# Batching two chunks of a spectral filter's last stage at the border of a step

## The chip, the cores and the metric

One core of one Trainium2 chip. The metric is the device time of one execution in microseconds, lower is better; the median of the runs is taken.

## What is computed

A global filter along the sequence (a real Fourier transform of 3008 points, a product with a filter, the inverse transform), and behind it a dense layer with a hard-swish and a second dense layer, all in fp32:

```python
X = np.fft.rfft(x, axis=1)                      # x: (8, 3008, 256)
Y = X * (filt_r + 1j * filt_i)[None, :, :]
x = np.fft.irfft(Y, n=3008, axis=1).reshape(24064, 256)
h = x @ w_in                                    # (256, 2048)
g = h * np.clip(h + 3.0, 0.0, 6.0) / 6.0
return g @ w_out                                # (2048, 256)
```

## The kernel before

**The two parts.** The 24064 tokens are 47 blocks of 512, which the kernel keeps as 256 pairs (a row and its mirror). For each block the dense layers run over eight slices of 256 hidden units. One slice of one block is a *step*; step 8k + p is slice p of block k. The Fourier stages of the next batch are woven between these steps: a hand-made plan (`at`, `plan`, `do`) says which unit runs at which step and at which of five places in it.

**A step.** In step i the kernel computes the hidden layer of slice p of block k (*up*) and the output products of the slice before (*down*). Both use a scheme with seven products in place of eight (a Strassen form). The tiles:

- *up*: PSUM banks `al` and `be`, one buffer each. `up_1` does three products (A11 into `al`, S1 and A12 into `be`), `up_2` S2 into `al` and S4 into `be`, `up_3` S3 into `al`, `up_5` A22 into `al`. In between, ScalarE copies `al` and `be` out, and VectorE forms the hidden values h0 (`up_2b`, L1007) and h1 (`up_3`, L1012); the last quarter of h1 is a ScalarE copy out of `al` (L1021). ScalarE takes the relu (L1026), VectorE the rest of the hard-swish into `g` (L1031), and three operations make the sums of `g` (`g_sums` L1038, L1039, `g_last` L1044).
- *down*: seven products, numbered 1 to 7, accumulate into four banks po0 to po3 (1 and 4 into po0, 2 and 6 into po1, 5 into po2, 7 and 3 into po3) over the eight slices of a block. Products 1, 2, 5 and 7 open their banks at slice 0. The preceding block's sums are taken out of the banks by `out_1` to `out_5`: ScalarE empties po0, VectorE po1 (`out_2`), one half of po3 (`out_3`), po2 (`out_4`, L1143 and L1144) and the other half of po3 (`out_5`, L1148). `out_4` and `out_5` run in the step with p = 1, in which slice 0 of the new block goes down.

All products go through `strips` (L972): two 64-column halves of the array for each.

**The border of a step.** A plain step issues up_1, place 0, down 1, up_2, down 2 and 4, up_3, down 5 and 6, up_5, down 7 and 3. Where a unit of the transform stands in place 3 (`a8_unit`, `b8_unit`, `bi8_unit`, 32-row shape, banks `al`, `be` and both of the pool psF), the step begins with this unit, and the order is another: unit, down 1, 2 and one half of 4, up_1, S2, the rest of 4 and one half of 5, S4, S3, the rest of 5, 6, 7, A22, 3.

**The last stage of the transform.** The last inverse stage makes the dense layers' input. It runs in *chunks* of five groups (`n_five`: 40 matmuls L899 with 48 rows, four tiles of 64 x 64 of the array at once, into two banks of psF) and of one or two groups (`n_unit`: through `strips`). A chunk reads a half of the tile `t4`, loaded from `g_tmp` by `t4_load` (SP queue), and ScalarE copies the result to the ring `xn` (`ring`, L872), which holds three blocks. A batch between the first and the last has seven chunks, q = 0 to 6: six of five groups and one of two. Before, each chunk runs by itself in place 0, behind up_1; a chunk of one or two groups that shares a step with a five uses unused halves of `al` and of po2 (`spare`). When a block is complete, `ready` plans the sums for the tile `xt` that the up products read: on POOL (`t_sums`), or as ScalarE copies and DMA adds on the POOL queue (`t_copy` L953, `t_add` L958).

Of the kernel before, what the change touches and what calls it, by code (L numbers as in the profile page):

```python
# [10 lines left out]
FP32 = mybir.dt.float32  # L11
I32 = mybir.dt.int32
AXT = mybir.ActivationFunctionType
# [14 lines left out]
NA = 47  # L28
NC = 64
KH = 24  # L30
NF = N // 2 + 1
P = 128
# [24 lines left out]
NBLK = B * N // BLK  # L57
NJ = 5
PAIRS = BLK // 2
RING = 3 * PAIRS  # L60
ND = (NJ + 1) * TOK
NX = PAIRS - NJ * NA
ATOM = 2 * KH
# [166 lines left out]
def kernel(  # L230
# [62 lines left out]
    ones = wai[:, HC * NA:].rearrange("p (s n) -> p s n", s=2)  # L293
    edge = wai[:, ds(2 * (NJ + 1) * NA, ND)]
    edges = edge.rearrange("p (j n) -> p j n", n=TOK)
    wi = const.tile([P, 3, NC], FP32, name="wi")
    wi2 = const.tile([P, 2, HC], FP32, name="wi2")
    xs = const.tile([P, 3, XC, D], FP32, name="xs")
    ft_all = const.tile([P, FB * TC, D], FP32, name="ft")
    ft = [ft_all[:, ts(i, TC), :] for i in range(FB)]  # L300
    t4 = const.tile([P, 2 * NJ, D], FP32, name="t4")
    xn = const.tile([P, 2, 2, RING], FP32, name="xn")
    w_all = const.tile([P, NP, 2, 7, P], FP32, name="w_all")
    w_in, w_out = ([w_all[:, p, i, :, :] for p in range(NP)] for i in range(2))
    b12 = const.tile([P, P], FP32, name="b12")
# [230 lines left out]
        nc.sync.dma_start(x0[X0:XR, j:j + n, :].rearrange("p j d -> p (j d)"), raw(x[0], j, [[HC * D, XR - X0], [1, n * D]]))  # L536

    def zt(dh):
        return (xn.rearrange("p a c n -> p (a c n)"), xs.rearrange("p i j d -> p (i j d)"))[dh]

    def copy(dve, to, ps):
        if dve:
# [290 lines left out]
    def pair(i):  # L833
        b, js, o, n = chunks[i]
        return b * HC * NA + o, n
# [28 lines left out]
                                              ap=[[D, KH], [step * 2 * KH * D, m], [1, D]]))  # L864
                    q += m

    def ring(i, a, m_, to, out, src):
        done = 0
        while done < m_:
            r = (chunks[i][0] * HC * NA + to + done) % RING  # L870
            m = min(m_ - done, RING - r)
            nc.scalar.activation(out=out(ds(r, m)), in_=src[:, :, ds(a + done, m)], func=AXT.Copy)  # L872
            done += m

    def ready(i):
        t, n = pair(i)
        k = t // PAIRS
        if (t + n) // PAIRS > k > 0:
            if n_at[i] % NP == 1 and k - 1 in kinds:
                st["xt", k] = xtp.tile([P, 5, PAIRS], FP32, name="xt")  # L880
                b = 4 + (kinds[k - 1] == "x")
                for j, (step, place_) in enumerate(((1, 1), (2, 0), (2, 1), (2, 1), (2, 2), (2, 2), (b, 1), (b, 1))):
                    plan.setdefault((n_at[i] + step, place_), []).append((t_copy if j < 4 else t_add, (k, j % 4)))
            else:
                t_sums(k)


    def n_five(i, ends_step=False):
        b, js, o, n = chunks[i]
        s0 = i % 2 * NJ  # L890
        banks = [psU.tile([P, 512], FP32, name=x) for x in ("al", "be")] if ends_step else [
            psF.tile([P, 512], FP32, name="psn", tag="f") for c in range(2)]
        ps = [t[:, 0:2 * n].rearrange("p (e n) -> p e n", e=2) for t in banks]
        for q, j in enumerate(js):
            for dh in range(2):
                for g in range(2):
                    for c in range(2):
                        r = ds(c * HALF, ATOM)
                        nc.tensor.matmul(ps[c][ts(g, HALF), dh, ts(q, NA)], t4[r, s0 + q, ds(dh * P + g * HALF, HALF)],  # L899
                                         groups[r, j, :], start=True, stop=True)  # L900
        for c in range(2):
            ring(i, 0, n, o, lambda at_: xn[:, :, c, at_], ps[c])
        ready(i)

    def n_unit(i, dh):
        if spare[i]:
            ps = st["po", n_at[i] // NP][2][:, 1, :, :].rearrange("p u m -> p (u m)") if dh else st["al"][:, 256:512]
        else:
            ps = psF.tile([P, 512], FP32, name="psn", tag="f")
        b, js, o, n = chunks[i]  # L910
        for q, j in enumerate(js):
            w = edges[0:2 * ATOM, FIRST.index(j), :] if i >= TAIL and j else ones[0:2 * ATOM, j, :]
            strips(ps[:, ts(q, TOK)], t4[0:2 * ATOM, i % 2 * NJ + q, ts(dh, P)], w, start=not spare[i], stop=True)
        for q, a, m, to in TO.get(i, [(q, 0, NA, o + q * NA) for q in range(len(js))]):
            ring(i, a, m, to, lambda at_: xn[:, dh, :, at_], ps[:, ts(q, TOK)].rearrange("p (c n) -> p c n", c=2))
        if dh:
            ready(i)


    def direct(i):  # L920
# [11 lines left out]
    def n_first():  # L932
        for (c, dh), ps in st.pop("psn").items():
            for q, j in enumerate(chunks[c][1]):
                strips(ps[:, ts(q, TOK)], t4[:, j - 1, ts(dh, P)], edges[:, FIRST.index(j), :], start=False, stop=True)
            to = xn[:, dh, :, 0:PAIRS]
            if c == 0:
                nc.scalar.activation(out=to[:, :, 0:NJ * NA].rearrange("p h (j a) -> p j h a", a=NA),
                                     in_=ps[:, 0:NJ * TOK].rearrange("p (j h a) -> p j h a", j=NJ, h=2), func=AXT.Copy)
                continue  # L940
            nc.scalar.activation(out=to[:, :, NJ * NA:], in_=ps[:, 0:2 * NX].rearrange("p (h a) -> p h a", h=2), func=AXT.Copy)
            nc.scalar.activation(out=xn[:, dh, :, ds(PAIRS, NA - NX)],
                                 in_=ps[:, 2 * NX:TOK].rearrange("p (c a) -> p c a", c=2), func=AXT.Copy)

    def xb(k, d, c):
        return xn[:, d, c, ts(k % 3, PAIRS)]

    F1, F3, F5, F2, F4 = range(5)

    def t_copy(k, j):  # L950
        t, (s0, s1) = st["xt", k], (xb(k, d, 1) for d in range(2))
        f, n, s, scale = ((F1, 2, s0, -1.0), (F5, 1, s0, 1.0), (F2, 1, s1, 1.0), (F4, 1, s1, -1.0))[j]
        nc.scalar.activation(out=t[:, f:f + n, :], in_=s.unsqueeze(1).broadcast_to([P, n, PAIRS]), func=AXT.Copy, scale=scale)  # L953
# [6 lines left out]
    def t_sums(k):  # L960
        t = xtp.tile([P, 5, PAIRS], FP32, name="xt")
        c0, s0, c1, s1 = (xb(k, d, c) for d in range(2) for c in range(2))
        u, v = (t[:, i, :] for i in (F5, F3))
        f1, f2, f3, f4, f5 = (t[:, i, :] for i in (F1, F2, F3, F4, F5))
        for o, x0, x1, op_ in ((f1, c0, s0, ALU.subtract), (u, c0, c1, ALU.add), (v, s0, s1, ALU.add),
                               (f4, u, v, ALU.subtract), (f5, u, v, ALU.add), (f2, c1, s1, ALU.add), (f3, f1, f2, ALU.add)):
            nc.gpsimd.tensor_tensor(out=o, in0=x0, in1=x1, op=op_)
        st["xt", k] = t

    def strips(ps, w, x, **kw):  # L970
        for o in range(0, P, STRIP):
            nc.tensor.matmul(ps[ds(o, STRIP)], w[:, ds(o, STRIP)], x, skip_group_check=True, **kw)  # L972
# [122 lines left out]
    def plain_up(p):  # L1095
        st["g", 0, p] = gp.tile([P, 7, 256], FP32, name="g")
        st["h"] = [psU.tile([P, 512], FP32, name=n) for n in ("al", "be")]
        for i in range(2):
            for d in range(2):
                strips(st["h"][i], w_in[p][:, 2 * d + i, :], xn[:, d, :, 0:PAIRS], start=d == 0, stop=d == 1)  # L1100
            relu(i)
            hswish(0, p, i)

# [96 lines left out]
    def at(step, fn, *a):  # L1200
        plan.setdefault((step, 0 if fn in EARLY else 1 if fn is w_scale else 2), []).append((fn, a))

    with tc.manual_schedule():
# [133 lines left out]
        at(0, wai_load)  # L1337
        at(2, x_load, 1, 2)

        n_at, spare = {0: -2, 1: -2}, {}  # L1340
        kinds = {}
        for n in range(2, B):
            for d, kind in enumerate("caxFFF"):
                kinds[first[n] - 7 + d] = kind

        N_AT = {"c": ((6, 6), (6, 6), (6, 6)), "F": ((1, 1), (1, 1), (6, 6)), "t": ((2, 4), (2, 4), (6, 6))}
        FIVE_AT = {"c": (6, 3, 6), "a": (1, 1, 5), "x": (1, 1, 5), "F": (1, 0, 1), "t": (4, 2, 4)}
        N_FIRST = {0: ((3, 4),), 1: ((), (2, 2), (3, 3)), 2: ((1, 1),), 3: ((1, 1),)}
        in_block = {}
        for i in range(2, len(chunks)):  # L1350
            in_block.setdefault(pair(i)[0] // PAIRS, []).append(i)
        stored = 0
        for i in range(2, len(chunks)):
            k = pair(i)[0] // PAIRS
            head = chunks[i][2] == 0
            same = in_block[k]
            at_, kind = same.index(i) + 1 if len(same) > 1 else 0, kinds.get(k - 1, "t")
            steps = N_FIRST[k - 1][at_] if k - 1 in N_FIRST else (FIVE_AT[kind][at_],) * 2 if len(chunks[i][1]) == NJ else N_AT[kind][at_]
            if head and len(same) == 1:
                steps = (6, 6)  # L1360
            s0, s1 = ((k - 1) * NP + s for s in steps)
            five = len(chunks[i][1]) == NJ
            n_at[i] = s1
            spare[i] = kind == "c" and at_ == 1
            if head:
                stored = s0 - 3 + (k == first[1])
            at(max(stored, n_at[i - 2] + 1), t4_load, i)
            if five:
                at(s1, n_five, i)
                continue  # L1370
            at(s0, n_unit, i, 0)
            at(s1, n_unit, i, 1)

        A_AT = (3, 10, 18, 21)
        SUM_AT = ((-10, -2), (2, 7), (13, 14), (15, 16))
# [219 lines left out]
```

## Time and profile before

| | us |
|---|---|
| median of 3 runs | 2537.55 (2536.87 to 2537.55) |
| the profiled execution | 2537.7 |
| its span, first to last instruction | 2535.8 |
| TensorE busy | 2521.5 |
| VectorE busy | 2012.9 |
| ScalarE busy | 1362.1 |
| GpSimd busy | 422.8 |

A row of the profile gives the line, the engine, the operation, what is written from what, the shape and the count; in the timeline each row begins with the start and the length in us from the start of the span. TensorE's matmul rows count each of the two passes of an fp32 matmul by itself. Matmuls overlap, so the length of one says less than the time from start to start. The granted clock was 1.0.

### The profile page before, as it was taken

How to read it: one execution, taken by the hardware profiler on the slowest of the kernel's cores; microseconds unless marked ns; L12 is line 12 of the kernel's file. 1: busy time of each engine (PE TensorE's matmuls, PEld its weight loads, DVE VectorE, ACT ScalarE, POOL GpSimd, SP SyncE). 2: the span in 40 equal slices, each digit the busy share in tenths (PEclk: the TensorE clock that was granted, in tenths of full speed). 3: DMA queues.
4: the chain of work that ended last, by engine and by line, in shares of the span. 5: the costliest groups of instructions: out<-in, count | busy, mean ns of one | idle time of the engine just before them, and what ended most of it. 6: DMA issues, size and time to landing. Idle time of an engine off the chain costs nothing.

```text
span 2535.8 us, 87287 instructions
## 1 busy us (share of the span) xinstructions
PE 2521.5 (99%) x37890; PEld 2007.3 (79%) x37890; DVE 2012.9 (79%) x3647; ACT 1362.1 (54%) x2836; POOL 422.8 (17%) x558
## 2 busy tenths in 40 slices
PE   8999999999999999999999999999999999999999
PEld 4478787887888788888888878887888878888887
DVE  6978888888787887878878788787887878766666
ACT  4554455555555555555555555555555555555554
POOL 3252111111211112111121111211102111011110
PEclk9999999999999999999999999999999999999999
DMA  8745556554445344443443443534424343211000
GB/s 239 235 123 165 162 138 155 160 136 101 118 98 137 99 102 121 98 129 99 112 121 86 132 109 98 135 89 117 121 68 96 88 103 91 53 41 26 19 22 26
DMA packets 210821, 276.91 MB, mean 109 GB/s; under 512 B 23274, under 2 KB 176392, under 8 KB 210054
## 3 DMA queue, kind: packets, MB, share of 16 engines
q1 hardware_dynamic: 163985, 200.75, 27.0%
q0 software_dynamic: 46112, 70.28, 14.2%
q8 instruction: 297, 4.87, 0.8%
q14 instruction: 86, 0.70, 0.1%
q10 hardware_dynamic: 341, 0.31, 0.1%
HBM read 164.38 MB, written 128.81 MB: 116 GB/s over the span
## 4 chain that ended last, share of the span: by engine, by line
PE 97%; DMA 1%; DVE 1%; SPq 0%; issue 0%; ACT 0%; DVEq 0%
PE po L972 46%; PE al L972 26%; PE be L972 19%; PE psn L899 2%; PE be L608 1%; PE al L779 1%; PE psf L706 1%; DMA bits<-in_moe_w_in_dram 0%; PE psf L693 0%; PE psf L589 0%; DMA w_all<-in_x_dram 0%; PE psf L763 0%; DMA zp_tmp<-y 0%; DMA w_all<-in_filt_r_dram 0%; PE po L685 0%
## 5 line engine op out<-in xcount | busy, mean ns | idle before, releaser
L972 PEld LDWEIGHTS po<-w_all,g 128*64 128x64 f32 x20808 | 1231.1, 137 | 263.0 <-issue 35.4
L972 PE MATMUL po<-w_all,g 128*64 128x128 f32 (+1 forms) x20808 | 1406.8, 274 | 0.3 <-DVE g L1031 0.3
L1026 ACT ACTIVATE r<-h,half_c 128x512 f32<-128x512 f32 x736 | 531.2, 722 | 335.9 <-DVE h L1007 323.8
L972 PE MATMUL al<-xt,w_all 128*64 128x256 f32 x4416 | 663.9, 379 | 0.1
L1031 DVE SCALAR_TENSOR_TENSOR g<-r,h 128x512 f32<-128x512 f32 x736 | 519.4, 706 | 146.9 <-ACT r L1026 133.5
L972 PE MATMUL be<-xt,w_all 128*64 128x256 f32 x2944 | 442.5, 379 | 0.0
L1007 DVE TENSOR_TENSOR h<-be,s 128x512 f32<-128x512 f32 x368 | 253.6, 689 | 169.8 <-PE be L972 138.0
L972 PEld LDWEIGHTS al<-xt,w_all 128*64 128x64 f32 x4416 | 285.1, 137 | 28.9 <-POOL w_all L469 1.0
L972 PEld LDWEIGHTS be<-xt,w_all 128*64 128x64 f32 x2944 | 209.0, 137 | 97.5
L1021 ACT ACTIVATE h<-al 128x256 f32<-128x256 f32 x368 | 141.0, 383 | 266.6 <-PE al L972 264.8
L1039 DVE TENSOR_TENSOR g<-g 128x512 f32<-128x512 f32 x367 | 255.6, 696 | 12.6
L1012 DVE TENSOR_TENSOR h<-al,s 128x256 f32<-128x256 f32 x368 | 155.6, 423 | 138.1 <-PE al L972 137.8
L972 PE MATMUL al<-xn,w_all 128*64 128x256 f32 (+1 forms) x1536 | 236.6, 388 | 1.0 <-DVE g L1031 0.5
L972 PE MATMUL be<-xn,w_all 128*64 128x256 f32 (+1 forms) x1536 | 236.4, 388 | 0.0
L991 ACT ACTIVATE s<-be 128x256 f32<-128x256 f32 x368 | 141.0, 383 | 148.9 <-PE be L972 145.9
L1002 ACT ACTIVATE s<-al 128x256 f32<-128x256 f32 x368 | 141.2, 384 | 124.2 <-PE al L972 121.0
L990 ACT ACTIVATE s<-al 128x256 f32<-128x256 f32 x368 | 141.5, 385 | 82.5 <-PE al L972 82.4
L1038 DVE TENSOR_TENSOR g<-g 128x256 f32<-128x256 f32 x367 | 162.1, 442 | 12.6
L1044 DVE TENSOR_TENSOR g<-g 128x256 f32<-128x256 f32 x367 | 155.4, 423 | 2.3
L972 PEld LDWEIGHTS be<-xn,w_all 128*64 128x64 f32 x1536 | 108.0, 137 | 53.4 <-issue 7.4
L958 POOL DMA_DIRECT2D xt<-xn x60 | 76.1, 1268 | 443.2 <-ACT xt L953 321.7
L1145 POOL TENSOR_TENSOR o<-p,o 128x256 f32<-128x256 f32 x45 | 33.0, 734 | 510.4 <-DVE o L1143 362.3
(206 smaller groups left out, 1976.9 us busy)
## 6 DMA issues: line engine op xcount, KB each, us to landing
g_tmp<-t POOLq DMA_DIRECT2D x96, 256.0 KB, 4.4
x_tmp<-in_x_dram SPq DMA_DIRECT2D x54, 384.0 KB
t<-g_tmp SPq DMA_DIRECT2D x168, 120.0 KB
ft<-f_tmp SPq DMA_DIRECT2D x36, 512.0 KB
t<-zp_tmp SPq DMA_DIRECT2D x36, 512.0 KB
o_tmp<-o SPq DMA_DIRECT2D x46, 256.0 KB
xt<-xn POOLq DMA_DIRECT2D x30, 384.0 KB, 6.2
zp_tmp<-y POOLq DMA_DIRECT2D x96, 96.0 KB, 3.7
```

The costliest lines, as they stand in the source:

```text
L972: nc.tensor.matmul(ps[ds(o, STRIP)], w[:, ds(o, STRIP)], x, skip_group_check=True, **kw)
L990: nc.scalar.activation(out=s[:, 0, :], in_=al, func=AXT.Copy)
L991: nc.scalar.activation(out=s5, in_=be[:, 1, :], func=AXT.Copy)
L1002: nc.scalar.activation(out=s[:, 1, :], in_=al, func=AXT.Copy)
L1007: nc.vector.tensor_tensor(out=st["h"][0].rearrange("p (a n) -> p a n", a=2), in0=be, in1=s, op=ALU.add)
L1012: nc.vector.tensor_tensor(out=st["h"][1][:, 256:512], in0=al, in1=s5, op=ALU.add)
L1021: nc.scalar.activation(out=st["h"][1][:, 0:256], in_=al, func=AXT.Copy)
L1026: nc.scalar.activation(out=r, in_=st["h"][i], func=AXT.Relu, bias=half_c, scale=1.0 / 6.0)
L1031: nc.vector.scalar_tensor_tensor(out=st["g", k, p][:, o:o + 2, :].rearrange("p a n -> p (a n)"), in0=st["r", i], scalar=1.0, in1=st["h"][i ...
L1038: v.tensor_tensor(out=g[:, G1, :], in0=g[:, G3, :], in1=g[:, G22, :], op=ALU.add)
L1039: v.tensor_tensor(out=g[:, G3:G2 + 1:2, :], in0=g[:, G3:G1 + 1, :], in1=g[:, G11:G11 + 1, :].broadcast_to([P, 2, 256]), op=ALU.subtract)
L1044: nc.vector.tensor_tensor(out=g[:, G4, :], in0=g[:, G12, :], in1=g[:, G2, :], op=ALU.subtract)
```

## The change

- The ring `xn` is split: the first part of the values (c = 0) keeps three blocks, the second (c = 1) gets four. `wi`, used at the start alone, now lies at the ring's end.
- In batches 1 to 6 the chunks q = 2 and 3 are one batch of ten groups (`n_ten`), and so are q = 4 and 5. The pair stands in place 3, at the border of a step: the first half goes to the two banks of psF, the second to `al` and `be`. The pairs are at steps 49, 65, 97, 113, 145, 161, 193, 209, 241, 257, 289 and 297, all with p = 1; one chunk of each pair was at that step before (in place 0), the other seven or eight steps later (in the pair at 257 one step earlier).
- In batches 1 to 4 the two-group chunk q = 6 and the first five of the next batch run together at the border of a step with p = 6 (`n_mixed`; the five goes to `al` and `be`), where they ran one behind the other inside the step.
- Other chunks run by themselves as before; the halves of `al` and po2 are no longer used. The one-group chunk of batch 0 moves from step 38 to 33.
- `ring` copies the two parts one by one, since their places in the ring differ; `ready` and `in_sums` plan the sums of each block that is complete, at the steps of before.

After the change the lines are shifted: `strips` is L1000, the five-group matmuls L905, h0 L1035, h1 L1040 and L1049, relu L1054, hard-swish L1059, `out_4` L1171 and L1172, `out_5` L1176, the ring's copies L875.

```diff
-RING = 3 * PAIRS
+RINGS = 3 * PAIRS, 4 * PAIRS
...
-    xn = const.tile([P, 2, 2, RING], FP32, name="xn")
+    xn = const.tile([P, 2, sum(RINGS)], FP32, name="xn")
...
-    def ring(i, a, m_, to, out, src):
-        done = 0
-        while done < m_:
-            r = (chunks[i][0] * HC * NA + to + done) % RING
-            m = min(m_ - done, RING - r)
-            nc.scalar.activation(out=out(ds(r, m)), in_=src[:, :, ds(a + done, m)], func=AXT.Copy)
-            done += m
+    def ring(i, a, m_, to, d, src):
+        for c in range(2):
+            done = 0
+            while done < m_:
+                r = (chunks[i][0] * HC * NA + to + done) % RINGS[c]
+                m = min(m_ - done, RINGS[c] - r)
+                nc.scalar.activation(out=xn[:, d, ds(c * RINGS[0] + r, m)], in_=src[c][..., ds(a + done, m)], func=AXT.Copy)
+                done += m
...
+    def n_ten(i):
+        out_ = five(i, [psF.tile([P, 512], FP32, name="psn", tag="f") for c in range(2)])
+        more = five(i + 1, [psU.tile([P, 512], FP32, name=x) for x in ("al", "be")])
+        out_()
+        more()
+        ready(i, 2)
...
+    def n_mixed(i):
+        ps = psF.tile([P, 512], FP32, name="psn", tag="f")
+        outs = [unit(i, ps[:, ds(dh * 2 * TOK, 2 * TOK)], dh) for dh in range(2)]
+        outs.append(five(i + 1, [psU.tile([P, 512], FP32, name=x) for x in ("al", "be")]))
+        for out_ in outs:
+            out_()
+        ready(i, 2)
...
+        N_FIRST = {2: (3, 4), 3: (10, 10), 4: (11, 11), 5: (17, 17), 6: (25, 25), 7: (33, 33)}
+        FIVE_AT = 6, 9, 17, 17, 33, 33, 41
+        TAIL_AT = (6, 6), (10, 10), (12, 12), (20, 20), (28, 28), (34, 36), (42, 44)
...
+            elif q == 6 and b < 5:
+                s0 = s1 = (first[b + 2] - 7) * NP + 6
+                mixed[i] = s1
+            elif b < B - 1:
+                s0 = s1 = (first[b + 1] - 7) * NP + FIVE_AT[q] - 8 * (b == B - 2 and q in (4, 5))
+                if q in (2, 4):
+                    tens[i] = s1
...
+            if i in tens:
+                plan.setdefault((s1, 3), []).append((n_ten, (i,)))
+            elif i in mixed:
+                plan.setdefault((s1, 3), []).append((n_mixed, (i,)))
+            elif i - 1 in tens or i - 1 in mixed:
+                continue
```

## The prediction

> **What bounds the kernel now.** I read the page's busy times and its chain first.
>
> ```profile
> PE 2521.5 (99%) x37890; PEld 2007.3 (79%) x37890; DVE 2012.9 (79%) x3647; ACT 1362.1 (54%) x2836; POOL 422.8 (17%) x558
> ...
> PE 97%; DMA 1%; DVE 1%; SPq 0%; issue 0%; ACT 0%; DVEq 0%
> ```
>
> TensorE carries the end: only what shortens, lengthens or stops its stream counts. A busy share hides short stops, since matmuls overlap, so I then read the starts of its instructions in the timeline. In the plain products they keep a fixed beat: two column halves start 7 ns apart, a 128-column pair takes 109.4 ns to the next, a 256-column pair 215.9 ns (one product 0.432 us, the first four passes of one `down` number 0.437 us). Anything over the beat is a stop. Over the whole trace almost all stops stand where the array changes its tile shape. Here is TensorE around one five-group chunk (start, length, then line, tile, shape, count):
>
> ```profile
> 510.40 0.60 PE L972 MATMUL be<-xn,w_all 128*64 128x256 f32 x4
> 510.83 0.60 PE L972 MATMUL be<-xt,w_all 128*64 128x256 f32 x4
> 511.37 1.38 PE L899 MATMUL psn<-wai,t 48*64 48x47 f32 x80
> 512.68 0.66 PE L972 MATMUL po<-w_all,g 128*64 128x128 f32 x8
> 513.16 0.60 PE L972 MATMUL al<-xt,w_all 128*64 128x256 f32 x4
> ```
>
> By the beat the chunk would start at 511.27; it starts 0.10 later. Its 80 passes are 20 waves of 58.4 ns, 1.17 us, but the next product comes 1.31 us after its start, 0.14 more; and that product's first wave takes 160 ns and not 109, 0.05 more. So one visit to the 48-row shape costs 0.29 us besides its work; all 46 chunks show these numbers. VectorE, ScalarE and the DMA queues stop TensorE hardly anywhere once the stream runs. One such stop shows how it is paid (VectorE's `g`, then TensorE waiting for it):
>
> ```profile
> 440.88 0.60 PE L972 MATMUL be<-xt,w_all 128*64 128x256 f32 x4
> ...
> 441.01 0.68 DVE L1031 SCALAR_TENSOR_TENSOR g<-r,h 128x512 f32<-128x512 f32 x1
> ...
> 441.75 1.09 PE L972 MATMUL po<-w_all,g 128*64 128x128 f32 x16 [0.27 <-DVE g L1031]
> ```
>
> VectorE ends at 441.692, TensorE goes on 0.054 us later, 0.43 after its beat, and its next wave is again 0.05 long. The ready product behind did not go first.
>
> **What goes.** The pairs (q 2 with 3, q 4 with 5 of batches 1 to 6) are 12, so 12 visits to the 48-row shape fall away: 12 x 0.29 = 3.5 us off. The chunks' 80 passes each stay. The four mixed batches (a two-group chunk, then a five) had one visit before and have one after (the two-group chunk has the plain 64-column shape): nothing. One wait goes: in step 38 the old chunk of one group waited 0.22 us for a copy out of `al`; it now runs alone in psF at step 33: 0.2 us off.
>
> **What moves onto the border of a step.** At a border step the order of the products is the one that the transform units use: chunk, down 1, 2 and half of 4, all three of up_1, S2, the rest of 4 and half of 5, S4, S3, rest of 5, 6, 7, A22, 3. Two differences from a plain step matter: product 7 comes before A22 and not after it, and only product 3 is left between A22 and the next step.
>
> All 12 pairs stand at steps with p = 1 (49, 65, 97 ...). No unit stood at p = 1 before. There the running block's slice 0 goes down, and product 7 opens bank po3, which still holds the preceding block's product 3 until `out_5` (VectorE, L1148 before, L1176 after) has read it. The built order of the changed kernel says the same: product 7 waits for `out_5`, and VectorE has in its queue h0, h1, out_5, g_last. When VectorE gets there is read from the transform border steps, which have the same TensorE order:
>
> ```profile
> 522.42 0.60 PE L972 MATMUL al<-xt,w_all 128*64 128x256 f32 x4
> ...
> 522.70 0.69 DVE L1007 TENSOR_TENSOR h<-be,s 128x512 f32<-128x512 f32 x1 [1.60 <-PE be L972]
> 522.85 1.26 PE L972 MATMUL po<-w_all,g 128*64 128x128 f32 x20
> 523.31 0.42 DVE L1012 TENSOR_TENSOR h<-al,s 128x256 f32<-128x256 f32 x1
> ...
> 523.64 0.42 DVE L1044 TENSOR_TENSOR g<-g 128x256 f32<-128x256 f32 x1
> ```
>
> From the start of S3 (522.42): h0 starts 0.286 later, h1 at 0.895, the next VectorE operation at 1.226. So it was in 54 of 63 such steps. In the pair's step that next operation is `out_5`, 0.415 us long: it ends at 1.641, and TensorE may go on at 1.695. Product 7 is due after S3 (0.432), half of 5 (0.219) and 6 (0.437), at 1.088. TensorE stops for 0.61 us, and the wave after it costs 0.05: 0.66 a pair, 12 x 0.66 = 7.9 us on. Behind the waiting product are A22 and 3, nothing of which hides it. In the plain step p = 1 before, this does not show:
>
> ```profile
> 515.55 0.42 DVE L1012 TENSOR_TENSOR h<-al,s 128x256 f32<-128x256 f32 x1 [0.54 <-PE al L972]
> ...
> 515.89 0.41 DVE L1148 TENSOR_TENSOR o<-po,o 128x256 f32<-128x256 f32 x1
> ...
> 516.21 0.60 PE L972 MATMUL al<-xn,w_all 128*64 128x256 f32 x4
> ...
> 516.64 1.04 PE L972 MATMUL po<-w_all,g 128*64 128x128 f32 x16
> 516.85 0.38 ACT L1021 ACTIVATE h<-al 128x256 f32<-128x256 f32 x1 [1.09 <-PE al L972]
> 517.27 0.72 ACT L1026 ACTIVATE r<-h,half_c 128x512 f32<-128x512 f32 x1
> ...
> 517.61 0.62 PE L706 MATMUL psf<-t,wa 32*32 32x512 f32 x2
> ```
>
> `out_5` ends at 516.31 and product 7 (the first of the x16) starts at 516.64.
>
> **The next border.** Every pair is followed at once by a transform unit (step 50, 66 ...), which also writes `al`. Above, the copy out of `al` ends 0.60 us after the products behind A22 start (517.236 less 516.637), and the unit comes 0.97 after it, since 7 and 3 lie between. With 3 alone the unit is due at 0.44 + 0.10 = 0.54, and the copy lets it go at 0.65: 0.11 us each, 1.3 us on. hswish of h1 then ends 2.08 after the same point, free for use at 2.13; down 2 comes at 0.65 + 1.07 (unit) + 0.49 (down 1) = 2.21: no further stop, but only 0.08 to spare.
>
> **The chunk's own waits.** In the second half of a pair TensorE takes two or more waits on `t4` loads in the middle of 58-ns waves. The loads are issued 7 steps and more ahead, some 45 us, so they are long landed, but each separate wait takes 0.051 us in the trace's queue rows. Before, they stood under the change of shape and cost nothing seen; two of them uncovered would be 0.1. No row shows them inside fast waves, so 0 to 0.1 each, middle 0.05: 0.6 us on.
>
> **What I cost at nothing.** *Copies to `xn`*: 54 more ScalarE instructions. The last chunks' small copies start 0.05 to 0.15 us apart, so eight more add 0.4 us to a step; the copy of S2's sum behind them has then about 0.4 us left before S3 needs it. In a pair, the copies of the first half run while the second half computes; `al` is copied 0.30 to 0.86 us after the last wave starts and is needed at 1.32, `be` is copied by 1.32 and needed at 1.75 (copies of this size follow at 0.46). A split where the ring ends adds 0.05. *Sums for `xt`*: 16 blocks get them from POOL and 30 from ScalarE copies with DMA adds, as before, at the same steps. *Loads and stores*: as many, SP's waits as far ahead as before. *Steps that lose a chunk* (57, 73 ...): step 81 of before is such a step (p = 1, no chunk, a transform two steps earlier) and shows no stop; its `out_5` ends 0.33 before product 7. *Longer rings*: they allow the earlier write, and no instruction of the stream reads them otherwise.
>
> **Sum.** The profiled execution took 2537.7 us (span 2535.8 and 1.9 around it), 0.15 over the median of 2537.55. -3.5 - 0.2 + 7.9 + 1.3 + 0.6 = +6.1: 2543.8 by the profile, 2543.6 by the median, 0.24% slower. About 0.2%, 5.1 us, is what a measurement of this kernel can tell from no change.
>
> **Rivals.** *A, not slower: product 7 does not hold TensorE up.* Either A22 and 3 pass it, or VectorE reaches `out_5` by 1.03 us after S3's start, the point from which it decides. Then the 7.9 goes: -3.5 - 0.2 + 1.3 + 0.6 = -1.8, 2535.7. Against it: the stop at 441.75, and the place of `out_5` behind h1, which needs S3. Chance 0.12. *B: ScalarE's copies come too late.* If the four copies of a pair only start when both halves are done, `al`'s is the third: free at 0.30 + 2 x 0.46 + 0.56 + 0.05 = 1.83 against 1.32, then `be` 0.03 more, so 0.54 x 12 = 6.5 on top, 2550. For it: copies of a chunk before start only 0.30 us after its last wave. Against it: the first half's banks are complete 1.2 us before the second's. [...] By this case's rows 0.4 us remain, so I don't take it. Chance 0.08. *C: the visits don't get cheaper*, if the change of bank inside a pair stops the waves as a new shape does: 3.5 comes back, 2547.1. Against it: inside a chunk the waves alternate two banks without a gap. Chance 0.05.
>
> **Range and chances.** The forecast has 0.75. Its unknowns: VectorE may start h1 0.25 sooner than in the model steps and the other two added waits vanish (12 x 0.41 - 3.7 = +1.2, 2538.7); or each restart shows a whole weight load (0.13) and the separate waits cost 0.1 (2546). With C and half of B inside, 2538.5 to 2548. Slower by over 0.2% means over 2542.6: about 0.55 of the forecast's 0.75, with B and C 0.68; within 0.2%, the rest of the forecast and A, 0.30; faster by over 0.2% would need 5.1 us where 3.7 at most can go, 0.02.
>
> **What would show it.** In the trace after: 34 visits to the 48-row shape; at each of the 12 pairs one entry and one exit of the old size around 160 passes; in the same step TensorE idle about 0.6 us before a `po` product, released by VectorE's `o` at L1176; a stop of about 0.1 at the next transform unit, released by ScalarE's h at L1049. Wrong if product 7 follows 6 on the beat, if `al` or `be` of up_1 waits for `xn` copies, or if stops appear in steps 57 or 73.

## The result, and the profile after

The changed kernel takes 2564.36 us (median of 4 runs, 2561.45 to 2567.98) against 2537.55 us before: 1.0104 times as long, 95% interval 1.0092 to 1.0117, or 26.8 us more. Forecast were 2543.6, range 2538.5 to 2548.0. The direction was right; the size was wrong by more than a factor of four.

The profiled execution, the longest of the four, took 2567.98 us (span 2566.2). From its page, the busy times and the chain of waits by engine:

```profile
PE 2530.7 (99%) x37890; PEld 2018.1 (79%) x37890; DVE 2006.6 (78%) x3647; ACT 1367.2 (53%) x2890; POOL 417.6 (16%) x558
...
PE 95%; DVE 2%; DMA 2%; issue 1%; SPq 0%; ACT 0%; DVEq 0%
```

TensorE runs as many matmuls as before (37890) and still carries the end, but VectorE, DMA and "issue" have taken 2 points of the chain from it. What TensorE waited for, after (view of waits, engine PE: us in total, times, the longest):

```profile
PE psn L905 <- DMA t<-g_tmp: 5.5, 2, 5.0
PE po L1000 <- DVE o L1176: 5.2, 12, 0.4
PE al L905 <- issue: 4.9, 4, 1.5
...
PE be L905 <- issue: 2.5, 3, 1.4
PE po L1000 <- issue: 2.2, 3, 1.1
```

None of the first four rows stands in the same view of before. (Of the fifth, one stop of 1.1 us at the start does.) The second row is the forecast one. The other two kinds were not forecast at all.

**The forecast stop.** The timeline of TensorE in the second pair's step after (start, length, line, tile, shape, count), then VectorE's:

```profile
527.72 0.60 PE L1000 MATMUL al<-xt,w_all 128*64 128x256 f32 x4
528.15 0.82 PE L1000 MATMUL po<-w_all,g 128*64 128x128 f32 x12
529.41 0.66 PE L1000 MATMUL po<-w_all,g 128*64 128x128 f32 x8 [0.44 <-DVE o L1176]
529.90 0.60 PE L1000 MATMUL al<-xn,w_all 128*64 128x256 f32 x4
...
530.87 0.62 PE L708 MATMUL psf<-t,wa 32*32 32x512 f32 x2
530.99 0.61 PE L708 MATMUL al<-t,wa 32*32 32x512 f32 x1
```

```profile
528.00 0.69 DVE L1035 TENSOR_TENSOR h<-be,s 128x512 f32<-128x512 f32 x1 [3.03 <-PE be L1000]
528.61 0.41 DVE L1040 TENSOR_TENSOR h<-al,s 128x256 f32<-128x256 f32 x1
528.94 0.41 DVE L1176 TENSOR_TENSOR o<-po,o 128x256 f32<-128x256 f32 x1
```

S3 starts at 527.72. `out_5` starts 1.22 us later (the model had 1.226) and product 7 goes on at 529.41, 1.69 later (1.695). Read from the waves' starts, the stop is 0.59 to 0.61 us in each of the twelve steps, 7.25 us in all. At 530.87 the transform unit's bank psf starts, and its `al` 0.12 later: the small second wait, forecast as 0.11.

**A load that came late (142 us).** SP's queue, then the granted TensorE clock (PEclk) in three stretches, first of after, then of before:

```profile
127.09 0.56 SPq L494 DMA_DIRECT2D x_tmp<-in_x_dram  x1
134.72 0.38 SPq L1200 DMA_DIRECT2D o_tmp<-o  x1
135.14 6.08 SPq L1203 DMA_DIRECT2D out_dram<-o  x7
141.27 1.58 SPq L864 DMA_DIRECT2D t<-g_tmp  x4
```

```profile
135.00:142.00 7.00, 7.00 (x100) 1.00 0.20 64
142.00:149.00 7.00, 1.50 (x28) 0.90 0.54 150
149.00:156.00 7.00, 7.00 (x122) 0.62 0.58 192
```

```profile
135.00:142.00 7.00, 7.00 (x125) 1.00 0.23 68
142.00:149.00 7.00, 7.00 (x146) 1.00 0.56 161
149.00:156.00 7.00, 7.00 (x162) 1.00 0.39 115
```

(Columns: the stretch, its length, TensorE busy and its matmuls, granted clock, DMA share, GB/s.) The new plan has a rule for loads, of which the front part of this document shows nothing:

```
at(max(stored, n_at[i - 2] + 1, s0 - 8 if q == 5 else s0 - 2 if q == 1 else 0), t4_load, i)
```

For chunk 3 (batch 0, q = 1, used at step 10) it moves the load from step 0 to step 8. There SP stands for 7.3 us in front of a block's output store. The view of waits has it as

```profile
SPq L1200 <- ACT s L1018: 7.3, 1, 7.3
```

The releaser named is a ScalarE operation on `s`, but the store reads `o`, and ScalarE's copy of `po` into `o` (L1146) ends at 134.69, 0.03 us before SP goes on: SP waits for the output itself. Then it issues eight stores for 6.5 us, and only then, at 141.27, the load that TensorE wants at 142.4. In before SP waits for such an output too (6.5 us), but chunk 3's load has been issued by 79.1 us. TensorE idles 5.9 us at 142 to 148.5, and from 147.5 us on its clock is granted at half for 6.8 us. The step is 8.7 us longer than before. In the later batches the same rule causes no stop.

**Stops with no releaser, in and behind the pairs.** The timeline of TensorE in a pair at 733 us (rows of single waves), and the clock around it:

```profile
732.83 0.23 PE L905 MATMUL be<-wai,t 48*64 48x47 f32 x1
732.88 0.23 PE L905 MATMUL al<-wai,t 48*64 48x47 f32 x1
734.51 0.26 PE L905 MATMUL be<-wai,t 48*64 48x47 f32 x1 [1.40 <-issue]
734.51 0.26 PE L905 MATMUL al<-wai,t 48*64 48x47 f32 x1
```

```profile
732.00:739.00 7.00, 5.60 (x114) 0.76 0.12 40
```

The waves come 58 ns apart and then not for 1.6 us. "issue" means that the profile shows nothing that TensorE waited for. Eleven of the twelve pairs have such a stop, of 0.2 to 1.7 us, some in the pair, some in the first products behind it; together 10.6 us over the beat, read from start to start (the view of waits lists less, since it counts idle time only). Two things tie them together. If all of TensorE's records in the trace are counted, the semaphore and drain records of its sequencer among them, the first late record of each of the eleven has a number that leaves 193 when divided by 256. (Without those few records the remainder drifts.) And the page of after has this queue:

```profile
q8 instruction: 297, 4.87, 0.8%
```

4.87 MB in 297 packets is 16.4 KB a packet, and TensorE's 76144 records divided by 297 are 256 a packet. The packet before the stop at 732.88 starts at 731.67 and takes 1.40 us; TensorE goes on 2.84 us after its start (2.3 to 2.9 at the eleven stops). Products of 128 columns use 36 records in a us, so a block of 256 of them lasts 7 us; the median of all blocks in after is 8.9. A pair is 320 records in 2.33 us: a block lasts 1.9. If TensorE needs the packet to go on, it matters where a pair lies in the count. At these stops the packet starts 0.1 to 1.2 us after TensorE passes 193 in the block before. If two such places fall into a pair and the products beside it, they are 1.8 to 3.0 us apart by the beat, and by this reading the block isn't there in time. In before no two such places are closer than 4.3 us. That these packets bring TensorE's next block is read from the counts and times; no row says so.

So there were three theories for the 26.8 us: (1) the late load, (2) product 7 behind `out_5`, (3) instruction blocks that pairs use up faster than they arrive. The rival to 3 was that the pairs themselves wait (the second `t4` slot's loads, the banks `al` and `be`, the memory port).

### The profile page after: what moved, and what is told of

It reads as the page before. It is cut to its first block, busy times and chain, and to the rows that moved or that the text cites. A ratio compares the mean times of both kernels' runs of the same rounds, so it can differ in the third digit from the quotient of the medians.

```text
span 2566.2 us, 87318 instructions
## 1 busy us (share of the span) xinstructions
PE 2530.7 (99%) x37890; PEld 2018.1 (79%) x37890; DVE 2006.6 (78%) x3647; ACT 1367.2 (53%) x2890; POOL 417.6 (16%) x558
## 3 DMA queue, kind: packets, MB, share of 16 engines
q1 hardware_dynamic: 163985, 200.75, 26.8%
q8 instruction: 297, 4.87, 0.8%
## 4 chain that ended last, share of the span: by engine, by line
PE 95%; DVE 2%; DMA 2%; issue 1%; SPq 0%; ACT 0%; DVEq 0%
PE po L1000 45%; PE al L1000 25%; PE be L1000 19%; PE psn L905 2%; PE be L610 1%; PE al L781 1%; PE psf L708 1%; PE al L905 1%; DMA bits<-in_moe_w_in_dram 0%; PE psf L695 0%; DVE h L1035 0%; DMA w_all<-in_x_dram 0%; PE psf L591 0%; PE psf L765 0%; PE psn L1000 0%
## 5 line engine op out<-in xcount | busy, mean ns | idle before, releaser
L1000 PEld LDWEIGHTS po<-w_all,g 128*64 128x64 f32 x20808 | 1235.9, 137 | 273.8 <-issue 37.6
L1000 PE MATMUL po<-w_all,g 128*64 128x128 f32 (+1 forms) x20808 | 1413.4, 275 | 7.4 <-DVE o L1176 5.2
L1054 ACT ACTIVATE r<-h,half_c 128x512 f32<-128x512 f32 x736 | 531.3, 722 | 345.4 <-DVE h L1035 333.3
L1000 PE MATMUL al<-xt,w_all 128*64 128x256 f32 x4416 | 667.1, 380 | 0.4 <-issue 0.2
L1059 DVE SCALAR_TENSOR_TENSOR g<-r,h 128x512 f32<-128x512 f32 x736 | 516.7, 702 | 154.4 <-ACT r L1054 141.4
L1000 PE MATMUL be<-xt,w_all 128*64 128x256 f32 x2944 | 444.3, 379 | 0.0
L1035 DVE TENSOR_TENSOR h<-be,s 128x512 f32<-128x512 f32 x368 | 253.4, 689 | 208.8 <-PE be L1000 194.0
L1000 PEld LDWEIGHTS al<-xt,w_all 128*64 128x64 f32 x4416 | 287.8, 137 | 34.3 <-POOL w_all L471 1.0
L1000 PEld LDWEIGHTS be<-xt,w_all 128*64 128x64 f32 x2944 | 210.2, 137 | 94.5 <-ACT xn L875 0.2
L1049 ACT ACTIVATE h<-al 128x256 f32<-128x256 f32 x368 | 141.1, 384 | 262.1 <-PE al L1000 261.1
L1040 DVE TENSOR_TENSOR h<-al,s 128x256 f32<-128x256 f32 x368 | 155.5, 423 | 126.5 <-PE al L1000 126.4
L1000 PE MATMUL al<-xn,w_all 128*64 128x256 f32 (+1 forms) x1536 | 236.8, 388 | 1.0 <-DVE g L1059 0.5
L1000 PE MATMUL be<-xn,w_all 128*64 128x256 f32 (+1 forms) x1536 | 237.2, 388 | 0.0
L1030 ACT ACTIVATE s<-al 128x256 f32<-128x256 f32 x368 | 142.0, 386 | 130.8 <-PE al L1000 127.0
L1000 PEld LDWEIGHTS be<-xn,w_all 128*64 128x64 f32 x1536 | 108.8, 137 | 52.5 <-issue 8.2
```

Source lines behind the costliest of these rows:

```text
L1030: nc.scalar.activation(out=s[:, 1, :], in_=al, func=AXT.Copy)
L1035: nc.vector.tensor_tensor(out=st["h"][0].rearrange("p (a n) -> p a n", a=2), in0=be, in1=s, op=ALU.add)
L1040: nc.vector.tensor_tensor(out=st["h"][1][:, 256:512], in0=al, in1=s5, op=ALU.add)
L1049: nc.scalar.activation(out=st["h"][1][:, 0:256], in_=al, func=AXT.Copy)
L1054: nc.scalar.activation(out=r, in_=st["h"][i], func=AXT.Relu, bias=half_c, scale=1.0 / 6.0)
L1059: nc.vector.scalar_tensor_tensor(out=st["g", k, p][:, o:o + 2, :].rearrange("p a n -> p (a n)"), in0=st["r", i], scalar=1.0, in1=st["h"][i ...
```

## Experiments, one cause at a time

**e1_load: chunk 3's load back at step 0.**

```diff
-... s0 - 2 if q == 1 else 0), t4_load, i)
+... s0 - 2 if q == 1 and b else 0), t4_load, i)
```

> The changed kernel with one load put back: the t4 load of chunk 3 (batch 0, used at step 10) is issued at step 0 again and not at step 8. Theory 1 (the moved load costs about 8.7 us: TensorE waits 5.9 us for it at 142 to 148 us, then runs at half clock for 7 us): the wait at 142 us and the half clock behind it vanish, 8.5 to 10 us less than the changed kernel's 2564.4, so 2554 to 2556; all stops later in the stream stay. Rival (early DMA traffic is full either way, so the load is only exchanged for another late one): less than 3 us less, another wait on a load between 100 and 160 us.

Measured: 2555.11 us (2552.31 to 2557.45), 9.3 under the changed kernel; 1.0069 of before (1.0054 to 1.0084). The stretch that was broken:

```profile
142.00:149.00 7.00, 7.00 (x144) 1.00 0.53 155
149.00:156.00 7.00, 7.00 (x163) 1.00 0.35 111
```

No stop, full clock, as before. Theory 1 holds.

**e2_out5: VectorE's `out_5` ahead of h0 and h1 in border steps.**

```diff
+    def out_5_add(k):
...
                 out_4(kd - 1)
+                if units:
+                    out_5_add(kd - 1)
             if up:
                 up_2b(k, p)
```

(`out_5_add` is the add alone; `out_5` then only stores.)

> The changed kernel with out_5's VectorE add issued ahead of h0 and h1 in every step that ends in a chunk or transform unit; the store stays where it was. Theory 2 (product 7 waits for out_5 only because VectorE does h0 and h1 first): the twelve stops of 0.6 us before the po product at L1000 vanish, 7.3 to 7.9 us less than the changed kernel, 2556.5 to 2557. Rival (something else releases product 7 just as late, or h0 and h1, now 0.42 us later, hold S3 or g up by as much): under 2 us less, with stops of about 0.4 us after S3 instead.

Measured: 2555.03 us (2553.49 to 2557.75), 9.3 under the changed kernel and so 1.5 more than the twelve stops and their slow first waves (7.9); the two medians come from different sets of runs, and single runs of the changed kernel spread over 6.5 us. The twelve stops are gone from the trace, and no wait has come in their place: h0 and h1 had 0.42 us to spare. Theory 2 holds.

**e3_pad: everything 164 records later.**

```diff
         keep_warm(2)
+        for i in range(41):
+            nc.tensor.matmul(ps[:, 0:16], zero[:, P:2 * P], zero[:, 0:16], start=True, stop=True)
```

> The changed kernel with 41 tiny matmuls (164 instructions) added to TensorE's stream at the very start, where it waits for the first loads anyway. Nothing else differs; every later instruction only stands 164 places later in the stream. Theory 3 (the stops of 0.2 to 1.7 us with no releaser in and behind the pairs are TensorE waiting for its next block of 256 instructions, because a pair uses up 320 instructions in 2.3 us; it depends on where the pair stands in its block): by the new places no pair should run out of instructions, these stops vanish, and the half clock at 734 us with them: 10 to 12.5 us less than the changed kernel, 2552 to 2554. Rival (they are waits of the pairs' own: separate t4 semaphores, the banks al and be, the memory port): no change, 2563 to 2566, with the stops at the same instructions.

Measured: 2565.14 us (2563.93 to 2568.35), no gain. Taken alone that speaks for the rival, but the trace does not: in none of the pairs is there a stop without a releaser, and of the new kinds of wait only the twelve at `out_5` and the late load are left. The time went at the start. Timeline of e3_pad there:

```profile
3.02 3.78 PE L1277 MATMUL al<-r 128*128 128x512 f32 x4 [3.02 <-ACT r L1272]
6.59 14.41 PE L1281 MATMUL al<-r 128*128 128x16 f32 x82
20.93 4.56 PE L1000 MATMUL po<-w_all 112*64 112x96 f32 x64
```

And TensorE's clock in the middle of the filling (columns: the stretch, its length, the busy time of the five engines, granted clock, DMA share, GB/s):

```profile
10.00:20.00 10.00, 10.00 (x53) 10.00 (x52) 0.00 (x0) 0.00 (x0) 0.00 (x0) 0.54 1.05 256
```

The 41 "tiny" matmuls took 14.4 us, and the first dense products start 14 us late. Up to about 10.8 us a pass of the filling takes 112 ns, although it moves only 16 columns; from there on the granted clock is half, and a pass takes 214. The first dense products are still slow behind it (64 matmul rows in 4.56 us, where after has 3.26). The edit was badly sized; theory 3 is not touched by it. **e4_all**, which has the same filling and the two edits above, suffers alike:

> The three edits together: the load of chunk 3 back at step 0, out_5 ahead of h0 and h1 in border steps, and the 41 tiny matmuls at the start. If the three causes are all there is and independent, what is left is the saving of the visits and the small terms: 2537.55 - 3.5 - 0.2 + 1.3 = 2535.2, up to 2537 with the separate t4 waits and the start. If a fourth cause is left, the time stays over 2539.

Measured: 2549.78 us (2547.30 to 2552.65). It is over 2539, but its trace shows no new stop in the pairs either, only the filling's 17.5 us at the start (all 82 passes 214 ns apart, here with a granted clock of 1.00 in the view of windows; why is not known).

**e7_pad4: the same shift, made cheap.**

```diff
-        keep_warm(2)
+        keep_warm(1)
+        ps2 = psU.tile([P, 512], FP32, name="be")
+        for i in range(42):
+            g, c, r = i // 2 % 2, i % 2, ds(i % 2 * HALF, ATOM)
+            nc.tensor.matmul((ps, ps2)[c][ts(g, HALF), 0:16], zero[r, ds(P + g * HALF, HALF)], zero[r, 0:16], start=True, stop=True)
```

> The 41 filling matmuls of e3_pad took 14.4 us at the start themselves (176 ns a pass with a full 128-column weight), which hid what they were for. Here 42 matmuls of 48 rows, 64 columns and 16 elements, spread over the four array tiles, take their place, and one of the two big warming matmuls at the start is left out for them: the same shift of 164 instructions for about 1.3 us less 1.1. Theory 3 (TensorE runs out of its block of 256 instructions in the pairs): the stops without a releaser vanish from the pairs, 10 to 12 us less than the changed kernel, 2552 to 2555. Rival (the pairs' own semaphores, banks or memory port): no change, 2563 to 2566. Already seen against the rival: in e3_pad the pairs had no such stop.

Measured: 2551.83 us (2551.02 to 2552.91), 12.5 under the changed kernel, 1.0054 of before (1.0040 to 1.0068). The waits of TensorE:

```profile
PE psn L905 <- DMA t<-g_tmp: 5.4, 2, 5.0
PE po L1000 <- DVE o L1176: 5.3, 12, 0.4
PE al L1277 <- ACT r L1272: 3.0, 1, 3.0
```

Causes 1 and 2 stand as they were; all "issue" rows of the pairs are gone. The pairs, their banks, loads and semaphores are the same; only their place in the count of records has moved, and no two places of 193 are closer than 3.2 us now. That excludes the rival.

**e9_before_pad4: the control, the kernel before with the same shift.**

> The kernel before with the same cheap shift at the start, a control. Theory 3: no chunk of 160 instructions outran its blocks in the kernel before at its old places, and none should at the new ones; only the shift's own cost shows, 2537 to 2539. If the time falls by several us, the shift does something else than move the pairs within their blocks.

Measured: 2537.02 us against 2538.27 of before in the same set of runs, ratio 0.9997 (0.9987 to 1.0006). The shift by itself does nothing.

**e5_double: the fast shape at length, without the change.** In before, each five-group chunk's matmuls are done twice in a row.

```diff
-        for q, j in enumerate(js):
+        for q, j in list(enumerate(js)) * 2:
```

> The kernel before with every five-group chunk's 40 matmuls done twice in a row, into the same banks: 320 instructions of the fast shape in one stretch, like a pair, but without al and be, without a second t4 slot and without any other part of the change. The arithmetic adds 46 x 1.17 = 53.8 us. Theory 3: on top come stops of 0.2 to 1.7 us with no releaser in those of the 46 stretches that stand badly in their blocks (about 15 to 22 of them by the places at which the changed kernel's pairs stopped), all at one and the same place of the 256: 11 to 25 us, 2602 to 2617 in all. Rival (banks al and be or the second t4 slot cause them): no such stop, 2590 to 2593.

Measured: 2614.8 us (two runs), 76.5 over before in the same set. Waits of TensorE, and the longest stop in the timeline:

```profile
PE psn L899 <- issue: 11.5, 12, 1.9
```

```profile
990.28 2.05 PE L899 MATMUL psn<-wai,t 48*64 48x47 f32 x126
994.21 0.26 PE L899 MATMUL psn<-wai,t 48*64 48x47 f32 x2 [1.88 <-issue]
```

Nineteen stops, 17.5 us over the beat, every one of them at 193 of 256 again and 2.2 to 2.9 us after the start of the last packet, in a kernel that has no pair, no `al` and `be` in a chunk and one `t4` slot a chunk. (At 740 us two such places are only 1.94 us apart and nothing stops: there the packet had started 0.5 us before the first of them.) 53.8 (the doubled work, from the expectation) + 17.5 are 71.3 of the 76.5. About 1.7 of the other 5 us is half clock behind the longest stop (3.4 us of it; granted 0.78 and 0.65 in the two stretches of 3 us from 994 us on); the rest is not assigned.

**e8_all4: the three edits, with the cheap shift.**

> The three edits together (chunk 3's load back at step 0, out_5 ahead of h0 and h1 in border steps, the cheap shift of 164 instructions). What is left of the change then is the saving of 12 visits (-3.5), the step-38 wait (-0.2), twelve waits of the transform unit for h1's copy (+1.3) and whatever the shift costs: 2535 to 2538. If a fourth cause is left, over 2539.

Measured: 2536.16 us (2534.85 to 2536.94) against 2538.27 in the same set, 0.9993 (0.9984 to 1.0002); and a second time:

> The kernel with all three edits a second time, beside the two others on the same chip, to compare with them: 2535 to 2537, and 0 to 2.5 us under the kernel before.

2536.49 us against 2537.96, 0.9994 (0.9985 to 1.0002). No further stop is left in the pairs' steps. What is left of the change is a gain that the measurement can't tell from nothing. It is a sum of small parts of both signs: step by step, the trace of e8_again is 1.4 us shorter than that of before, with 2.0 less in the twelve pairs' steps, 0.7 less in the steps before 40, 1.0 more in the four mixed batches (0.1 to 0.4 each) and 0.3 more at the start. In e8_all4 the four mixed batches also add 1.0; in one of them, at 967.7 us, product 3 waits 0.3 us for `g_last`. What holds up the other three is not known. One pair in e8_all4, which shows where it is (from the chunk's start to the first product behind it):

```profile
509.75 1.38 PE L905 MATMUL psn<-wai,t 48*64 48x47 f32 x80
```

```profile
512.23 0.55 PE L1000 MATMUL po<-w_all,g 128*64 128x128 f32 x6
```

2.48 us for 160 passes. A chunk alone takes 1.311 from its start to the next product, two 2.622: 0.14 saved, and the entry (0.10) and the slow first wave (0.05) once instead of twice. That is 0.29 a pair, as forecast, 3.5 in all; the 0.11 at the next border comes off it again.

**e10_two: the load and `out_5`, no shift.** Only cause 3 is left.

> The load and the out_5 edits without the shift, so that only the stops without a releaser are left of the three causes: 10 to 12.5 us over the kernel with all three edits, 2546 to 2548.7. If the causes overlap (a stop in one place taking up slack of another), it lies under 2546.

Measured: 2546.16 us (2545.15 to 2547.63), 9.7 over e8_again on the same chip; ten stops without a releaser add up to 8.8 in its trace. It lies at the lower edge of what was expected. So cause 3 is worth nearly 10 us by medians; the 12.5 of e7_pad4 against the changed kernel also holds the half clock at 734 us (some 1.7) and the spread between sets. For the same reason the three single gains (9.3, 9.3 and 12.5) add up to 31.1 and not to 26.8.

**e6_gap: the pair's halves apart.** As e10_two, but the second half in place 0 of the same step, in psF.

```diff
     def n_ten(i):
-        out_ = five(i, [... "psn" ...])
-        more = five(i + 1, [... "al", "be" ...])
-        out_()
-        more()
-        ready(i, 2)
+        five(i, [... "psn" ...])()
+    def n_more(i):
+        five(i + 1, [... "psn" ...])()
+        ready(i, 2)
...
+                plan.setdefault((s1, 0), []).append((n_more, (i,)))
```

> Load of chunk 3 back, out_5 ahead of h0 and h1, no shift; and the second half of each pair moved away from the first, to the place behind up_1 of the same step, in psF banks: 160 instructions at a time again. Theory 3: no stop without a releaser although nothing is shifted; the 12 visits to the 48-row shape come back (+3.5), the transform unit's wait for h1's copy goes (-1.3): 2.2 us over the kernel with all three edits, so about 2538.4. If visits in truth cost nothing, it would lie 1.3 under that kernel, at 2535; if the stops belong to something else in the pairs' steps than 320 instructions in a row, they stay, and it takes 2546 or more.

Measured: 2546.54 us (2544.92 to 2548.57), where 2538.4 was expected. By the number alone I would have had to say that the stops stay. They don't: the trace has no stop without a releaser from the first pair on. With 160 records at a time, unshifted, the blocks keep up; theory 3 holds. The time has gone into the new place. VectorE and TensorE there, then a weight load of S3 in the first pair's step:

```profile
404.49 1.22 DVE L524 TENSOR_TENSOR xs<-xs,wa 128x1024 f32<-128x1024 f32 x1
...
405.63 0.68 DVE L1059 SCALAR_TENSOR_TENSOR g<-r,h 128x512 f32<-128x512 f32 x1
...
406.46 0.88 PE L1000 MATMUL po<-w_all,g 128*64 128x128 f32 x12 [0.54 <-DVE g L1059]
```

```profile
411.40 0.20 PEld L1000 LDWEIGHTS al<-xt,w_all 128*64 128x64 f32 x4 [0.46 <-ACT s L1030]
```

In six of the twelve steps a VectorE operation of the transform (1.22 us) stands ahead of `g`, and the products that need `g` stop for 0.7 us each; before, product 2 and half of 4 ran later. The second half, between up_1 and S2, has an entry and an exit of its own, which add the 3.5. And in each of the twelve steps S3 waits for ScalarE's copy of S2's sum (L1030), which now comes behind the copies of the second half: S3 starts 0.55 or 0.61 us after S4 and not 0.43, and its next wave is slow, so about 0.20 is lost. 6 x 0.71 + 12 x 0.29 + 12 x 0.20 = 10.1, against 10.0 over e8_again. The expectation had costed the place at nothing. It had also taken 1.3 us off for the next unit's wait; that wait stayed, at 0.12 in all twelve steps.

**e11_seven and e12_best: product 7 behind A22 in the pairs' steps**, without and with the edit on `out_5` (load and shift as in e8_all4).

```diff
-                down(kd, pd, *((6, 7) if units else (6,)))
+                down(kd, pd, *((6, 7) if units and not after_up else (6,)))
...
-                down(kd, pd, *(() if units else (7,)), ...)
+                down(kd, pd, *(() if units and not after_up else (7,)), ...)
```

(`after_up` is true in the twelve steps.)

> The same without moving out_5: load back, shift, product 7 behind A22 in the pairs' steps. Product 7 is then due 1.088 + 0.43 = 1.52 us after S3's start and out_5 lets it go at 1.695: 0.17 + 0.05 in place of 0.66, and no wait of the unit: 12 x 0.22 = 2.6 over the kernel above, 2537.6. If the order of 6 and 7 is not what makes the wait long, the stops of 0.6 stay and it takes about 2543.

> All three edits, and in the steps that end in a pair product 7 goes behind A22 again as in a plain step (6, A22, 7, 3). Theory: with 7 and 3 both between A22 and the transform unit, the unit comes 0.97 us after A22 and no longer waits for h1's copy out of al: 12 x 0.11 = 1.3 us less than the kernel with the three edits (2536.2 and 2536.5), so 2535. Rival (the unit waits for something else than that copy, or A22, now earlier, waits itself): no gain or a loss of 1 to 3 us.

Measured: 2538.64 (2537.43 to 2539.85) and 2538.85 us (2537.47 to 2539.63), both 1.0006 of before (0.9997 to 1.0015). e11_seven came out 1 us over its number, and by another way; e12_best went the rival's way. TensorE and VectorE in a pair's step of e12_best:

```profile
515.91 0.60 PE L1000 MATMUL al<-xt,w_all 128*64 128x256 f32 x4
516.34 0.82 PE L1000 MATMUL po<-w_all,g 128*64 128x128 f32 x12
517.27 0.65 PE L1000 MATMUL al<-xn,w_all 128*64 128x256 f32 x4
```

```profile
516.81 0.41 DVE L1040 TENSOR_TENSOR h<-al,s 128x256 f32<-128x256 f32 x1
```

A22 (517.27) writes `al`, which h1 (to 517.22) still reads. By the beat it was due at 516.99; it waits 0.28 and pays the slow wave of 0.05, in both kernels: 12 x 0.33 = 3.9 us against the 1.3 saved, 2.6 net. Against the before of its own set each, e11 and e12 are 1.2 and 1.4 us slower where the two runs of e8 are 2.1 and 1.5 faster, a difference of 2.7 to 3.5 with intervals of some 2.3 either way. In e11_seven this wait also gives `out_5` the time that it needs, so product 7 doesn't stop at all. So product 7 ahead of A22 has a use: at a border it covers h1's read of `al`, and the transform unit's 0.12 us is its small price. So the border order is the common root of both forecast terms, but turning it back is no gain; `out_5` ahead of h0 is.

## Why the prediction was wrong, by its steps

- **What goes (-3.5 and -0.2).** The 3.5 was right: 2.48 us a pair against 2.62, entry and first wave once. (Not quite all 46 chunks of before show the model's numbers: two take 2.05 and 1.36 us. No pair hangs on it.) The steps before 40 gained 0.7 us in e8_again, more than the 0.2.
- **The four mixed batches ("nothing").** Wrong by a small term: +1.0 us in e8_all4 and in e8_again.
- **Product 7 behind `out_5` (+7.9).** Right in mechanism, place and size: 12 stops of 0.59 to 0.61 us and a slow wave each; taking them out was worth 8.9 (e10_two under e1_load) to 9.3 us by medians of different sets.
- **The next border (+1.3).** Right: 0.12 a unit against 0.11.
- **The chunk's own waits (+0.6).** Not there: ten of the twelve pairs in e8_all4 take 2.486 to 2.488 us and the other two 2.49 and 2.52, where 40 waves of 58.4 ns and the exit of 0.14 make 2.48. It was a small term, and the miss does not hang on it.
- **"Loads and stores: as many, SP's waits as far ahead as before."** This step failed, at +8.7 us. The number is the same, but one load was moved by eight steps, to two steps ahead of its use, past a block's output store on the same queue. The trace of before shows SP's issue of such stores and what it waits for, so the price could have been worked out; I costed all loads in one sentence instead. The sentence in the part on the chunk's own waits ("issued 7 steps and more ahead, some 45 us") holds for the pairs, not for this chunk.
- **No step for the supply of instructions.** This is the term that was missing, at 10.6 us in the trace of after and 9.7 by medians (e10_two over e8_again), and with it about 1.7 of half clock. The sum took a pair's matmuls to run at the beat of a single chunk's, because a chunk's waves do. In before the longest stretch of that beat was 160 records, and no row shows a stop; a stretch twice as long was outside of what the trace had shown, and the prediction should have said so and bounded it. What was to be had from before: a queue named "instruction" in the page, and 137 records a us in a chunk against 36 in products of 128 columns.
- **Rivals.** A (product 7 passes) fell by the twelve stops, C (visits no cheaper) by the 2.48 us, B (copies too late): no TensorE wait in a pair's step is released by an `xn` copy. None of the three was the miss.
- **The sum.** -3.5 - 0.2 + 7.9 + 1.4 = 5.6 by the prediction's own terms as measured, + 8.7 + 10.6 + 1.7 = 26.6. That this lies so close to the 26.8 of the medians is luck: the late load, the stops and the half clock are read from the profiled execution, whose trace is 30.4 us longer than that of before. Of the 3.8 us between, 1.0 each is in the mixed batches and in the start, 0.4 in a later wait for `g`, and 1.8 in the pairs' steps is not assigned; -0.5 is the earlier steps' further gain, and the rest is rounding. With the three causes out, e8 should lie at -2.3 by the first, second and fourth terms; measured were -2.1 and -1.5 us, with intervals of some 2.3 us either way. That too is in part luck, since +1.0 of the mixed batches and -0.7 of the early steps nearly cancel.
- **Chances.** 0.68 on slower was borne out, but on a sum that held less than a quarter of the loss.

## What to carry to other kernels

When a step is moved, follow every load that it moves to its queue and read there what the queue waits for and issues just ahead of it; "as many as before" is no cost. When a change makes a longer run of short, fast instructions than the trace has shown, bound what feeds them: compare instructions per us in the run (here 137) with what the instruction queue brings (here 256 records a packet), and if a stop has no releaser, count all records of the engine up to it, semaphore records too, modulo the records of a packet before looking for a semaphore. A fix can be as plain as a shift: here 42 small matmuls at the start took away nearly 10 us 400 to 2000 us later, but every later edit of the stream moves the pairs again, so the count has to be taken anew each time.

## What the chip showed that I had not expected

- At one place of a block of 256 records (193) TensorE stopped 30 times in after and e5_double, for 0.2 to 2.1 us, in stretches of 320 short records, and went on 2.2 to 2.9 us after the start of the last instruction packet. In before, which has no such stop, the packet starts at least 2.7 us ahead of that place, packets and places counted in order. The packets at these stops took 0.9 to 1.4 us, all packets of after 0.9 to 1.95. Once, in e2_out5 at 346 us, TensorE stopped for 0.7 us behind a single chunk of 160: the packet there had started 3.6 us after the place before, and why so late is not known.
- Behind some stops, not all, the granted clock falls to half: for 6.8 us from the end of the 5.9 us wait at 142 us, for 3.4 us after the 1.6 us stop at 733 us, and for 3.4 us after a stop of 1.4 at 1356 us in e1_load (granted 0.54 and 0.89 in the two stretches of 3 us from 1356 us on), while stops of 1.3 and 1.7 us at 416 and 1052 us in after leave it at 1. What decides which stop has half clock behind it was not tested.
- In e3_pad a matmul pass with a 128-column weight and 16 columns of data took 112 ns at full clock, and the granted clock fell to half at 10.8 us while TensorE was filled with such passes back to back; whether it was they that brought it down was not tested. The 42 matmuls of e9_before_pad4, with small weights spread over the array's tiles, cost nothing that the measurement shows (0.9997).
